# FNet mixing and a gated FFN on one core: first weight piece by halves, batch 0 folded row by row, piece 4 loaded behind slice 1's tables

## The chip, the cores and the metric

One core of a Trainium2 chip runs the whole program. The engines that matter: TensorE (PE) multiplies, with its weight loads shown apart as PEld; VectorE (DVE), ScalarE (ACT) and GpSimd (POOL) work element by element; SyncE (SP) does nothing but issue DMAs. Each engine takes its instructions in the order of the program and waits at the head of its queue. The metric is device time in microseconds of one execution, the median of several; lower is better.

## The reference

```python
def _attn_ref(x):                      # x: (8, 3008, 256)
    X = np.fft.fft(x, axis=1)
    X = np.fft.fft(X, axis=2)
    return X.real.astype(np.float32)

def _moe_ref(x, w_gate, w_val, w_out): # x: (24064, 256), d_ff = 1536
    gate = 1.0 / (1.0 + np.exp(-(x @ w_gate)))
    val = x @ w_val
    return (gate * val @ w_out).astype(np.float32)

def reference(**kwargs):
    ...
    attn_out = _attn_ref(**attn_kwargs)
    B, S, D = attn_out.shape
    x = attn_out.reshape(B * S, D)
    return _moe_ref(x=x, **moe_kwargs)
```

The weights arrive as float64 (8 bytes each), x as float32.

## The kernel before

The real part of the two-dimensional transform is a product with cosine and sine tables. Each batch of 3008 rows is first folded by its symmetries into four quarters (index h) of 126 x 6 points: 126 partitions, and six points per partition that the code calls rows, q = 0 to 5. The fold is additions and subtractions of quarters and of mirrored features. Six rows, taken two at a time, make three slices (N3 = 3) of batch 0; a slice is loaded by one DMA (`load_third`, 1 MB, tile x) and has two table parts (`load_table`, tile st, 0.38 MB each). The sums over rows run on TensorE with the folded rows as weights and the tables as the moving operand, into the PSUM tiles ev and od; a small extra sum for one feature column goes to the tile pe (`e0_sums`). The transform along the features is not carried out on x: it is multiplied into the gate and value weights instead ("merge", `dt` is its table, result G), so that afterwards the main loop works from pk and qk (the sums over rows), G and the output weights wf.

The weights are cut in 18 pieces of 256 x 256 float64 numbers, 0.5 MB each: pieces 0 to 11 alternate between gate and value, 12 to 17 belong to the output weights. A piece is loaded into raw (and its copies wqk, wf, wc, wx by home), as two 128-row blocks c = 0 and 1, side by side. It is converted to float32 by integer operations on the two 32-bit halves of each number:

- `weight_parts` (ScalarE): an Abs of the high words (L317) and a scaled Copy of the low words (L319);
- `weight_join`: on VectorE two tensor_scalar operations through a PSUM bank (L330, L331) and one scalar_tensor_tensor (L333), and an add on GpSimd (L335);
- `merge`: eight matmul instructions (four matmuls, each in two passes) into a PSUM bank ps, and `merged` copies that to G on ScalarE (L366). `ge_load` moves a row of G into the tile ge by small DMAs.

Order is by hand: the program schedules nothing by itself, every engine runs its instructions as they are written. SP issues, in this order: pieces 0 and 1, dt, pieces 2 and 3; then for each slice j its part of x, piece 3 + j if j > 0, and its tables; then pieces 6 and 7. The start proper is the part from `warm(12)` to `weight_join(5, "x2")`: twelve matmuls on a constant tile (busy), pieces 0 to 3 converted and merged, then the loop over the three slices. In a slice, `folds[2 * j]` is `third` (L506, L507, twice L468, on VectorE) with a copy to xe on ScalarE (L524), and `folds[2 * j + 1]` is `feats` (L513, L515, L516, on VectorE) with `turned` (L518, three copies a slice on ScalarE: XV, which lies in the tile st, and a copy within x for each row). The matmuls of the slice follow: e0 sums, halves 0 and 1 (ev and od of two blocks) first with the rows themselves and then with the turned copies, and the group halves[2]. Piece 4 is converted across slices 0 and 1 and merged behind slice 1; piece 5 is converted behind slice 1, its join behind the loop.

After the loop come the copies of the sums (`then` and `places`: a copy on ScalarE, L586, and two VectorE operations, L592 and L596), pieces 6 to 10 woven into another group of sums (ev and od, six matmul instructions at a time), the first `seed` and `front_a` calls, and the main loop of `front_a`, `front_b`, gate and `back`, which runs to the end.

Of the kernel before, what the change touches and what calls it, by code (L numbers as in the profile page):

```python
# [53 lines left out]
NQ = 6  # L54
# [28 lines left out]
def kernel(  # L83
# [50 lines left out]
    def mm(o, l, r, start, stop):  # L134
        nc.tensor.matmul(o, l, r, start=start, stop=stop, skip_group_check=True)  # L135
# [129 lines left out]
    def weight_load(j):  # L265


        w, c = jobs[j]
        src = (moe_w_gate, moe_w_val, moe_w_out)[w]
        src = src[2 * c * P : 2 * (c + 1) * P, :] if w == 2 else src[:, c * WC : (c + 1) * WC]  # L270
        src = src.rearrange("(c p) f -> p c f", p=P)

        def some(n, pool, tag):

            if tag not in shared:
                shared[tag] = pool.tile([P, n * WC], F32, name=f"w{tag}", tag=tag)
            return shared[tag]

        def home(j):

            if j in (0, 1, 2, 10, 11):
                t = hp.tile([P, 6 * WC], F32, name="raw", tag="h")
                return t[:, 0 : 4 * WC], t[:, 4 * WC :]
            if j in (3, 4):
                ws = some(5, pqp, "qk")[:, (j - 3) * 2 * WC : (j - 2) * 2 * WC]
                return sp.tile([P, 4 * WC], F32, name="raw", tag="sf"), ws
            if j < 8:
                t = wf[:, j - 4].rearrange("p m n -> p (m n)")
                return t[:, 0 : 4 * WC], t[:, 4 * WC : 6 * WC]
            if j < 10:  # L290
                shared[j] = cp.tile([P, 10 * WC], F32, name="wc", tag="c")
                return shared[j][:, 0 : 4 * WC], shared[j][:, 4 * WC : 6 * WC]
            return (shared[8][:, 6 * WC :] if j == 12 else shared["qk"][:, 0 : 4 * WC],
                    shared[9][:, (6 + 2 * (j - 12)) * WC : (8 + 2 * (j - 12)) * WC])

        if j < KEEP:
            raw, ws = home(j)
        else:
            both = some(24, xp, "x4").rearrange("p (i n) -> p i n", n=2 * WC)
            i = 3 * (j - KEEP)  # L300
            raw, ws = both[:, i : i + 2].rearrange("p a n -> p (a n)"), both[:, i + 2]
        raw = raw.bitcast(I32).rearrange("p (c f w) -> p c f w", c=2, w=2)
        ws = ws.rearrange("p (c f) -> p c f", c=2)
        WS[j] = ws
        if src.dtype == F32:
            nc.sync.dma_start(out=ws, in_=src)
        else:
            RAW[j] = raw
            nc.sync.dma_start(out=raw.rearrange("p c f w -> p c (f w)"), in_=src.bitcast(I32))  # L309

    def weight_parts(j, which=(0, 1)):

        if j in RAW:
            raw, ws = RAW[j], WS[j]
            lo, hi = raw[:, :, :, 0], raw[:, :, :, 1]
            if 0 in which:
                nc.scalar.activation(ws, hi.bitcast(F32), AF.Abs)  # L317
            if 1 in which:
                nc.scalar.activation(lo, lo.bitcast(U32), AF.Copy, scale=2.0 ** -29)  # L319

    def weight_join(j, other=None):
        if j not in RAW:
            return
        raw, ws = RAW.pop(j), WS[j]
        lo, hi = raw[:, :, :, 0], raw[:, :, :, 1]
        wi = ws.bitcast(I32)
        mid_ = bank("join", other).rearrange("p (c f) -> p c f", c=2)
        mi = mid_.bitcast(I32)
        ts = nc.vector.tensor_scalar
        ts(out=mid_, in0=ws, scalar1=2.0 ** -15, scalar2=HUGE, op0=ALU.max, op1=ALU.min)  # L330
        ts(out=mi, in0=mi, scalar1=3, scalar2=0x3FFFFFF8, op0=ALU.logical_shift_left,  # L331
           op1=ALU.bitwise_and)
        nc.vector.scalar_tensor_tensor(out=wi, in0=hi, scalar=-(2 ** 30), in1=mi,  # L333
                                       op0=ALU.bitwise_and, op1=ALU.bitwise_or)
        nc.gpsimd.tensor_tensor(wi, wi, lo, op=ALU.add)  # L335

    WO, parts_ = {}, []

# [14 lines left out]

    def merge(ws, g, c, other):
        ps = MERGED[g, c] = bank("ps", other)
        for h in range(2):
            for t in range(2):
                mm(ps[:, h * WC : (h + 1) * WC], dt[:, t, h * HD : (h + 1) * HD], ws[:, t, :],
                   h == 0 and t == 0, t == 1)

# [251 lines left out]

    E0 = {}

    def e0_sums(j, which=(0, 1)):

        for turned in which:
            for q in (2 * j, 2 * j + 1):
                for blk in range(2):
                    row = (2 * blk + q % 2) * TB  # L620
                    w = xe[:, blk, q : q + 1] if turned else W[0, blk][2][:, q]
                    mm(E0["ps"][row : row + 1, columns(blk)[turned]], w, table_of(0, q, blk, turned),
                       not j and not turned, j == N3 - 1)

    def e0_copies():

# [336 lines left out]
    def piece(j, other=None):  # L963
        merge(WS.pop(j), *jobs[j], other)
# [246 lines left out]
```

## Time and profile before

| what | value |
|---|---|
| device time, median of 3 | 1923.47 us (1922.28 to 1925.69) |
| profiled execution, its own time | 1922.13 us |
| its span, first to last instruction | 1920.4 us |
| granted TensorE clock | 1.000 |
| TensorE busy | 1911.3 us, 100% |
| VectorE, ScalarE, GpSimd busy | 74%, 70%, 81% |
| DMA, moved in all | 95.63 MB, mean 50 GB/s |
| DMA from 9 to 18 us, 18 to 26 us | 326 GB/s, 311 GB/s |

The first slices of the span are unlike the rest, in which TensorE is busy throughout and the DMA nearly idle:

| stretch, us | PE busy | DVE busy | ACT busy | POOL busy | DMA GB/s |
|---|---|---|---|---|---|
| 0 to 9 | 7.07 | 4.22 | 4.59 | 3.17 | 268 |
| 9 to 18 | 7.58 | 8.71 | 3.92 | 5.12 | 326 |
| 18 to 26 | 8.00 | 6.96 | 5.06 | 0.66 | 311 |
| 26 to 33 | 6.61 | 6.04 | 3.66 | 0.67 | 296 |
| 33 to 40 | 7.00 | 5.80 | 5.48 | 2.04 | 218 |
| 40 to 60 | 19.87 | 16.61 | 17.72 | 7.64 | 188 |

How to read it: an instruction's line in the timeline gives its start, its duration, the engine, the source line, what it writes and reads, how many were merged, and in brackets how long the engine was idle before and what released it. The ends of matmuls are modelled, so TensorE's busy time is not its work at its peak rate; the distance between starts is. All matmuls have one source line (L135, a helper), so they are told apart by tile.

### The profile page before, as it was taken

To read this page: it belongs to the slowest core of one execution; us is meant where nothing else is said; L and a number is where in the kernel's file an instruction comes from. 1 tells how busy PE (TensorE), PEld (TensorE's weight loads), DVE (VectorE), ACT (ScalarE), POOL (GpSimd) and SP (SyncE) were. 2 spreads that over 40 slices of the span, in tenths; PEclk is the share of its full clock that TensorE was granted. 3 is DMA by queue.
4 is the path that set the end of the run, shared out by engine and by line. 5 is a ranking of instruction groups with operands and counts; after the bars stand their busy time and mean duration, and the time that the engine had idled before them with its cause. 6 is when DMAs were issued, how large, how long until landed. Compare 5 with 4: busy or idle time off the path is not lost.

```text
span 1920.4 us, 34666 instructions
## 1 busy us (share of the span) xinstructions
PE 1911.3 (100%) x11342; PEld 1793.1 (93%) x11342; DVE 1411.7 (74%) x3216; ACT 1345.3 (70%) x3155; POOL 1555.5 (81%) x2811
## 2 busy tenths in 40 slices
PE   9999999999999999999999999999999999999999
PEld 7899999999999999999999999999999999999998
DVE  8667876787777876777777777777777687767776
ACT  6877767767777677776777767777677767777775
POOL 3589979978898688986888878988788876777775
PEclk9999999999999999999999999999999999999999
DMA  9342322120120201202111020111200100010001
GB/s 302 97 83 50 94 82 61 46 80 15 24 78 20 80 20 42 60 15 83 26 47 47 21 83 19 47 52 23 80 15 16 26 15 15 15 23 19 26 18 29
DMA packets 169299, 95.63 MB, mean 50 GB/s; under 512 B 129742, under 2 KB 160024, under 8 KB 167328
## 3 DMA queue, kind: packets, MB, share of 16 engines
q1 hardware_dynamic: 168838, 93.17, 17.6%
q8 instruction: 91, 1.49, 0.3%
q14 instruction: 88, 0.72, 0.1%
q10 hardware_dynamic: 250, 0.24, 0.0%
q0 software_dynamic: 32, 0.00, 0.0%
HBM read 68.13 MB, written 47.24 MB: 60 GB/s over the span
## 4 chain that ended last, share of the span: by engine, by line
PE 96%; DMA 2%; SPq 1%; POOL 0%; DVE 0%; ACT 0%; issue 0%; ACTq 0%; POOLq 0%
PE pf L135 50%; PE po L135 41%; PE ev L135 3%; PE rows L135 1%; DMA x<-in_xf_dram 1%; PE od L135 1%; DMA wc<-in_moe_w_out_dram 0%; DMA wx<-in_moe_w_out_dram 0%; PE row L135 0%; SPq L309 0%; POOL sf L773 0%; SPq L214 0%; PE pe L135 0%; PE ps L135 0%; POOL st L239 0%
## 5 line engine op out<-in xcount | busy, mean ns | idle before, releaser
L773 POOL TENSOR_TENSOR sf<-h 128x168 f32<-128x168 f32 (+1 forms) x935 | 516.4, 571 | 230.4 <-DVE h L767 229.6
L773 POOL TENSOR_TENSOR sf<-h,sf 128x168 f32<-128x168 f32 (+1 forms) x1122 | 614.9, 568 | 49.0 <-DVE h L767 48.0
L135 PE MATMUL pf<-pk,G 128*128 128x252 f32 (+1 forms) x2304 | 582.6, 376 | 0.0
L135 PE MATMUL pf<-qk,G 128*128 128x252 f32 (+1 forms) x2304 | 582.0, 375 | 0.1
L725 ACT ACTIVATE pf<-ek,ge 128x252 f32<-128x252 f32 (+1 forms) x1152 | 542.6, 471 | 19.5 <-DVE h L767 0.3
L767 DVE TENSOR_TENSOR h<-pf,z 128x252 f32<-128x252 f32 (+1 forms) x576 | 241.5, 419 | 413.3 <-ACT pf L764 411.8
L135 PE MATMUL po<-sf,wf 128*128 128x168 f32 (+1 forms) x2992 | 516.9, 306 | 0.3 <-POOL sf L773 0.2
L736 ACT ACTIVATE ae<-pf 128x504 f32<-128x504 f32 (+1 forms) x576 | 339.1, 589 | 247.0 <-PE pf L135 245.3
L135 PEld LDWEIGHTS pf<-pk,G 128*128 128x128 f32 x2304 | 436.8, 190 | 52.0 <-issue 2.0
L135 PEld LDWEIGHTS po<-sf,wf 128*128 128x128 f32 x2992 | 460.4, 190 | 9.2 <-POOL sf L773 1.2
L135 PE MATMUL po<-h,wf 128*128 128x168 f32 (+1 forms) x2618 | 463.2, 305 | 0.0
L135 PEld LDWEIGHTS pf<-qk,G 128*128 128x128 f32 x2304 | 410.6, 190 | 26.6 <-ACT ae L736 0.8
L751 DVE TENSOR_TENSOR z<-ae,pf 128x504 f32<-128x504 f32 (+1 forms) x576 | 386.0, 670 | 62.6 <-ACT h L750 58.0
L135 PEld LDWEIGHTS po<-h,wf 128*128 128x128 f32 x2618 | 416.5, 190 | 16.2
L891 DVE TENSOR_TENSOR c<-c 128x168 f32<-128x168 f32 (+1 forms) x929 | 425.6, 466 | 3.4
L750 ACT ACTIVATE h<-pf 128x252 f32<-128x252 f32 (+1 forms) x576 | 218.4, 379 | 208.1 <-PE pf L135 200.4
L763 DVE TENSOR_TENSOR h<-h,pf 128x252 f32<-128x252 f32 (+1 forms) x576 | 233.6, 405 | 0.0
L764 ACT ACTIVATE pf<-z 128x252 f32<-128x252 f32 (+1 forms) x576 | 211.4, 367 | 24.9 <-DVE h L763 21.0
L773 POOL TENSOR_TENSOR sf<-sf 128x168 f32<-128x168 f32 (+1 forms) x187 | 104.3, 558 | 14.7
L773 POOL TENSOR_TENSOR sf<-sf,h 128x168 f32<-128x168 f32 (+1 forms) x187 | 110.1, 589 | 0.0
L804 ACT COPY c<-po 128x504 f32<-128x504 f32 (+1 forms) x141 | 80.0, 568 | 0.0
L900 DVE STREAM_TRANSPOSE os<-c 128x256 f32<-128x256 f32 x184 | 79.9, 435 | 0.0
(163 smaller groups left out, 919.8 us busy)
## 6 DMA issues: line engine op xcount, KB each, us to landing
x<-xr SPq DMA_DIRECT2D x14, 1536.0 KB
out_dram<-os SPq DMA_DIRECT2D x368, 56.0 KB
xr<-in_xf_dram SPq DMA_DIRECT2D x14, 768.0 KB
xr<-in_xf_dram SPq DMA_DIRECT2D x35, 256.0 KB
ek<-ed SPq DMA_DIRECT2D x39, 126.0 KB
out_dram<-os SPq DMA_DIRECT2D x284, 7.0 KB
x<-in_xf_dram SPq DMA_DIRECT2D x3, 1024.0 KB
st<-in_stab_dram SPq DMA_DIRECT2D x4, 564.8 KB
```

Source lines behind the costliest of these rows:

```text
L135: nc.tensor.matmul(o, l, r, start=start, stop=stop, skip_group_check=True)
L725: nc.scalar.activation(PF[i][:, g], EK[i // NFT], AF.Copy, scale=ge[:, g, f : f + 1])
L736: nc.scalar.activation(AP[i], PF[i], AF.Copy, scale=2.0)
L750: nc.scalar.activation(H[p][:, fh, 0:n], PF[i][:, 0], AF.Sigmoid)
L751: nc.vector.tensor_tensor(z[:, :, ::-1], AP.pop(i), PF[i], op=ALU.subtract)
L763: nc.vector.tensor_tensor(h[:, fh, 0:n], h[:, fh, 0:n], pf[:, 1], op=ALU.mult)
L764: nc.scalar.activation(pf[:, 0], z[:, 0], AF.Sigmoid)
L767: nc.vector.tensor_tensor(h[:, fh, n:], pf[:, 0], z[:, 1], op=ALU.mult)
L773: nc.gpsimd.tensor_tensor(block(p, dst), block(p, a), block(p, b), op=(ALU.subtract, ALU.add)[op])
L804: (nc.vector.tensor_copy if t == 1 or t == 3 and not last else nc.scalar.copy)(C[0][:, 3 * t * R : 3 * (t + 1) * R], PO[t][:, 0 : 3 * R])
L891: engine.tensor_tensor(t[:, dst * R : (dst + 1) * R], *v, op=(ALU.subtract, ALU.add)[op])
L900: nc.vector.transpose(os_[0][:, s, 0:nb, h, :], t[:, c0 : c0 + nb * TB])
```

## The change

The edits, all in the start of the kernel:

1. Piece 0 is loaded by two DMAs, one for each 128-row block, and converted block by block on all engines.
2. In pieces 1 to 4 the last two steps of the join (L333 on VectorE and the add on GpSimd) are done block by block; the steps ahead of them stay whole.
3. The matmuls of a merge run block by block (t outside, h inside), for all pieces.
4. Batch 0 is folded and summed row by row (six steps) instead of by slices of two rows (three steps); `e0_sums` takes one row.
5. Piece 4 is loaded behind slice 1's tables instead of ahead of them, and converted and merged as a whole behind row 3. The first ScalarE step of piece 5 runs behind row 4, the second behind row 5.
6. Twelve warm-up matmuls become nine.

```diff
         WS[j] = ws
+        cuts = (slice(0, 1), slice(1, 2)) if not j else (slice(0, 2),)
         if src.dtype == F32:
...
         else:
             RAW[j] = raw
-            nc.sync.dma_start(out=raw.rearrange("p c f w -> p c (f w)"), in_=src.bitcast(I32))
+            for c in cuts:
+                nc.sync.dma_start(out=raw[:, c].rearrange("p c f w -> p c (f w)"),
+                                  in_=src[:, c].bitcast(I32))
...
-    def weight_join(j, other=None):
+    def weight_join(j, other=None, cuts=(BOTH,), last=None):
...
-        ts(out=mid_, in0=ws, scalar1=2.0 ** -15, scalar2=HUGE, op0=ALU.max, op1=ALU.min)
-        ts(out=mi, in0=mi, scalar1=3, scalar2=0x3FFFFFF8, op0=ALU.logical_shift_left,
-           op1=ALU.bitwise_and)
-        nc.vector.scalar_tensor_tensor(out=wi, in0=hi, scalar=-(2 ** 30), in1=mi,
-                                       op0=ALU.bitwise_and, op1=ALU.bitwise_or)
-        nc.gpsimd.tensor_tensor(wi, wi, lo, op=ALU.add)
+        for c in cuts:
+            w, m = ws[:, c], mid_[:, c]
+            ts(out=m, in0=w, scalar1=2.0 ** -15, scalar2=HUGE, op0=ALU.max, op1=ALU.min)
+            m = m.bitcast(I32)
+            ts(out=m, in0=m, scalar1=3, scalar2=0x3FFFFFF8, op0=ALU.logical_shift_left,
+               op1=ALU.bitwise_and)
+            for d in last or (c,):
+                wi, lo, hi = ws[:, d].bitcast(I32), raw[:, d, :, 0], raw[:, d, :, 1]
+                nc.vector.scalar_tensor_tensor(out=wi, in0=hi, scalar=-(2 ** 30), in1=mid_[:, d].bitcast(I32),
+                                               op0=ALU.bitwise_and, op1=ALU.bitwise_or)
+                nc.gpsimd.tensor_tensor(wi, wi, lo, op=ALU.add)
...
-        for h in range(2):
-            for t in range(2):
+        for t in range(2):
+            for h in range(2):
                 mm(ps[:, h * WC : (h + 1) * WC], dt[:, t, h * HD : (h + 1) * HD], ws[:, t, :],
                    h == 0 and t == 0, t == 1)
...
-    def e0_sums(j, which=(0, 1)):
-
-        for turned in which:
-            for q in (2 * j, 2 * j + 1):
-                for blk in range(2):
...
+    def e0_sums(q, turned):
+
+        for blk in range(2):
...
     for j in range(N3):
         load_third(j)
-        if j:
-            weight_load(3 + j)
+        if j == N3 - 1:
+            weight_load(5)
         for t in range(2):
             load_table(t, j)
+        if j == 1:
+            weight_load(4)
...
-    warm(12)
+    warm(9)
     for j in range(4):
-        weight_parts(j)
-        weight_join(j, j % 3)
+        weight_parts(j, cuts=(BOTH,) if j else HALVES)
+        weight_join(j, j % 3, (BOTH,) if j else HALVES, HALVES if j else None)
         piece(j, ("x0", "x1", "x2", 3)[j])
...
-    folds = fold_ops(0, 2)
+    folds = fold_ops(0, 1)
...
-    for j in range(N3):
-        qs = (2 * j, 2 * j + 1)
-        folds[2 * j]()
-        if not j:
-            e0_sums(j)
+    for q in range(NQ):
+        folds[2 * q]()
+        e0_sums(q, 0)
+        if not q:
             merged(3)
             ge_load(3)
             for i in (8, 9, 10, 11, 12):
                 weight_load(i)
-        else:
-            e0_sums(j, (0,))
-        if j == N3 - 1:
-            merged(4)
-        folds[2 * j + 1]()
-        for sums, _, _ in halves[0:2]:
-            sums(*qs, which=(0,))
-        if j:
-            e0_sums(j, (1,))
-        for sums, _, _ in halves[0:2]:
-            sums(*qs, which=(1,))
-        halves[2][0](*qs)
-        if j == 0:
-            weight_parts(4)
-        elif j == 1:
-            weight_join(4, "x2")
-            piece(4, "x2")
-            weight_parts(5)
+        folds[2 * q + 1]()
+        for sums, _, _ in halves[0:2]:
+            sums(q, which=(0,))
+        e0_sums(q, 1)
+        for sums, _, _ in halves[0:2]:
+            sums(q, which=(1,))
+        halves[2][0](q)
+        if q == 3:
+            weight_parts(4)
+            weight_join(4, "x2", last=HALVES)
+            piece(4, "x2")
+        elif q == 4:
+            merged(4)
+            weight_parts(5, (0,))
+    weight_parts(5, (1,))
     weight_join(5, "x2")
```

`weight_parts` takes the same cuts and runs its two ScalarE operations for each. HALVES are the slices 0:1 and 1:2 of the block index, BOTH is 0:2.

More of the change, by code (lines that the diff above doesn't have):

```diff
@@ L304, in weight_load, with weight_parts @@
         WS[j] = ws
+        cuts = (slice(0, 1), slice(1, 2)) if not j else (slice(0, 2),)
         if src.dtype == F32:
-            nc.sync.dma_start(out=ws, in_=src)
+            for c in cuts:
+                nc.sync.dma_start(out=ws[:, c], in_=src[:, c])
         else:
             RAW[j] = raw
-            nc.sync.dma_start(out=raw.rearrange("p c f w -> p c (f w)"), in_=src.bitcast(I32))
-    def weight_parts(j, which=(0, 1)):
-        if j in RAW:
[L314 to L319, printed above, removed]
-    def weight_join(j, other=None):
+            for c in cuts:
+                nc.sync.dma_start(out=raw[:, c].rearrange("p c f w -> p c (f w)"),
+                                  in_=src[:, c].bitcast(I32))
+    BOTH = slice(0, 2)
+    HALVES = (slice(0, 1), slice(1, 2))
+    def weight_parts(j, which=(0, 1), cuts=(BOTH,)):
+        if j in RAW:
+            for c in cuts:
+                raw, ws = RAW[j][:, c], WS[j][:, c]
+                lo, hi = raw[:, :, :, 0], raw[:, :, :, 1]
+                if 0 in which:
+                    nc.scalar.activation(ws, hi.bitcast(F32), AF.Abs)
+                if 1 in which:
+                    nc.scalar.activation(lo, lo.bitcast(U32), AF.Copy, scale=2.0 ** -29)
+    def weight_join(j, other=None, cuts=(BOTH,), last=None):
         if j not in RAW:
@@ L324, in weight_join @@
         raw, ws = RAW.pop(j), WS[j]
-        lo, hi = raw[:, :, :, 0], raw[:, :, :, 1]
-        wi = ws.bitcast(I32)
         mid_ = bank("join", other).rearrange("p (c f) -> p c f", c=2)
-        mi = mid_.bitcast(I32)
         ts = nc.vector.tensor_scalar
-        ts(out=mid_, in0=ws, scalar1=2.0 ** -15, scalar2=HUGE, op0=ALU.max, op1=ALU.min)
-        ts(out=mi, in0=mi, scalar1=3, scalar2=0x3FFFFFF8, op0=ALU.logical_shift_left,
-           op1=ALU.bitwise_and)
-        nc.vector.scalar_tensor_tensor(out=wi, in0=hi, scalar=-(2 ** 30), in1=mi,
-                                       op0=ALU.bitwise_and, op1=ALU.bitwise_or)
-        nc.gpsimd.tensor_tensor(wi, wi, lo, op=ALU.add)
+        for c in cuts:
+            w, m = ws[:, c], mid_[:, c]
[8 more added lines that the diff above has]
+                nc.gpsimd.tensor_tensor(wi, wi, lo, op=ALU.add)
     WO, parts_ = {}, []
@@ L613 @@
     E0 = {}
-    def e0_sums(j, which=(0, 1)):
-        for turned in which:
-            for q in (2 * j, 2 * j + 1):
-                for blk in range(2):
[L620 to L623, printed above, removed]
+    def e0_sums(q, turned):
+        for blk in range(2):
+            row = (2 * blk + q % 2) * TB
+            w = xe[:, blk, q : q + 1] if turned else W[0, blk][2][:, q]
+            mm(E0["ps"][row : row + 1, columns(blk)[turned]], w, table_of(0, q, blk, turned),
+               q < 2 and not turned, q >= NQ - 2)
     def e0_copies():
```

## The prediction

> **What bounds the kernel now.** I read the page first, for the busy shares and the chain that ended last; then the chain in order of time for the first 100 us; then the timeline from 0 to 75 us, engine by engine; last the busy time by windows, for the DMA rate.
>
> The page, its busy line and the chain by engine:
>
> ```profile
> PE 1911.3 (100%) x11342; PEld 1793.1 (93%) x11342; DVE 1411.7 (74%) x3216; ACT 1345.3 (70%) x3155; POOL 1555.5 (81%) x2811
> ...
> PE 96%; DMA 2%; SPq 1%; POOL 0%; DVE 0%; ACT 0%; issue 0%; ACTq 0%; POOLq 0%
> ```
>
> TensorE holds 96% of the chain. The matmuls of the main loop are the same before and after, so the change can move the end only by moving the moment from which TensorE runs without a break. The chain in order of time shows where that moment is:
>
> ```profile
> 11.68 14.87 DMA x<-in_xf_dram
> 26.57 0.17 DVE x L506
> 26.74 1.14 DVE x L507
> 27.91 0.70 DVE x L468
> 28.63 0.69 DVE x L468
> 29.32 0.04 issue
> 29.37 0.69 DVE x L515
> 30.08 0.70 DVE x L516
> 30.78 0.04 issue
> 30.83 0.59 PE ev L135 x2
> ```
>
> The last third of batch 0 (x2) lands at 26.57, VectorE folds both its rows until 30.77, and TensorE starts their sums at 30.83. From there the weight loads wait 0.30, 0.31 and 0.53 us (at 41.44, 47.62, 56.62), and next to nothing until the tail. So the end is 30.83 plus the work behind it. The batch-0 sums end at 35.39, when the next group (ev x6) starts; I follow that mark. The timeline also shows what VectorE and GpSimd do to each other:
>
> ```profile
> 13.97 1.21 DVE L507 TENSOR_TENSOR x<-x 126x1020 f32<-126x1020 f32 x1
> 14.09 2.23 POOL L335 TENSOR_TENSOR wqk<-wqk,raw 128x512 int32<-128x512 int32 x1 [0.78 <-ACT G L366]
> 15.21 2.38 DVE L468 TENSOR_TENSOR x<-x 126x512 f32<-126x512 f32 x2
> ...
> 25.34 1.29 POOL L335 TENSOR_TENSOR wqk<-wqk,raw 128x512 int32<-128x512 int32 x1 [9.03 <-DVE wqk L333]
> ```
>
> The same GpSimd add takes 1.29 alone and 2.23 beside the fold; the two L468 take 2.38 instead of 1.42 (at 20.28). About 0.95 is lost on each side.
>
> **Part by part.** *Prices on VectorE.* 126x1020 takes 1.21, 126x508 0.68: 1.04 ns an element and 0.15 fixed. A dependent next operation starts 0.03 after the end of the one before (28.63, 29.37, 30.08), an independent one 0.08 before it (30.69 after an end at 30.77). So 256 elements take 0.42, as L763's 128x252 does (0.41), and start to start 0.455 or 0.34.
>
> *Loads.* Piece 0 as two transfers is one more issue of 0.45 on SP; everything on SP goes out 0.5 later until 6.55, where an issue already takes 2.54 because the queue is full, so nothing later moves. Piece 4's 0.5 MB and slice 1's tables change places, both still ahead of x2, so x2 lands at 26.57 again. The tables land some 1.5 earlier. Piece 4 lands near 23 instead of by 20.50 (the tables' 0.76 MB at the 190 to 300 GB/s of that stretch); ScalarE asks for it at 25.5, so 2 us cover that. Piece 5 keeps its place.
>
> *Pieces 0 to 3.* The first half lands between 3.9 and 4.9; by its bytes 4.3. VectorE starts at 4.8 instead of 5.63. Piece 0 costs six operations, 2 x (0.455 + 0.455 + 0.34) = 2.5 instead of 2.07; pieces 1 to 3 cost 0.725 x 2 + 0.34 x 2 = 2.13 each. VectorE is free at 4.8 + 2.5 + 6.4 = 13.7, where it was 13.89: gain 0.2. TensorE's piece 3 ends two halves sooner (GpSimd's 128x256 add is 0.73 in the trace), near 16.3 instead of 18.1. That alone shortens nothing: the rows come from VectorE. The swapped loops of the merge and warm(9) move no matmul onto the path.
>
> *Row by row.* One row: 0.08 + 0.72 + 3 x 0.455 + 0.34 = 2.5 on VectorE. Before, a slice took 18.96 to 23.07, 2.06 a row. So 0.45 more for each of six rows. [...]
>
> Rows 0 and 1: 13.7 + 5.0 + 0.9 beside GpSimd's add of piece 3 (paid before too) = 19.6; x1 had landed by 18.96. Rows 2 and 3 end at 24.7.
>
> *Piece 4, moved.* Its ScalarE parts are queued behind row 3's xe, XV and turned copy, which wait for row 3's last VectorE operation. The two copies start 0.40 apart each (0.89 for two now), so Abs runs 25.5 to 26.2. VectorE stands behind that: join(4) is ahead of row 4 in its queue, so it idles 24.7 to 26.2 and joins until 28.35. Before, join(4) ran at 23.07 and was over at 25.2, ahead of x2's landing. Now row 4 starts 1.8 after x2 landed. GpSimd's add of piece 4 ran at 25.34, while VectorE idled; its second half now meets row 4. That costs VectorE between 0 and 0.97 (the row at 15.21); I take 0.75, one half add. [...] Rows 4 and 5 then end at 28.35 + 0.75 + 5.0 + 0.1 = 34.2, instead of 30.77: 3.4 later.
>
> *TensorE behind it.* A row's sums: six matmuls in two passes, 8 x 0.16 for halves 0 and 1, 4 x 0.16 for the third, 0.1 at each change of shape: 2.1. The e0 sums ran as 8 instructions in 0.43, four column groups side by side; by row only two stand side by side: 0.21 to 0.43 for 4, I take 0.32, twice a row. Together 2.75 a row, 5.5 a slice where it was 4.7. Piece 4's matmuls stand ahead of row 4 on TensorE and end near 31. Row 4 can start at 31.8 and ends near 34.2; row 5's e0 goes first, its sums follow feats at 34.3 to 34.5, and all end at 37.0. Before: 35.39. So **+1.6 us**: of the 3.4 VectorE loses, 1.8 come back because only one row's sums, not two, stand behind its end.
>
> *After that.* ScalarE's four row-wise extras per slice (0.2 to 0.4 each) lie in its idle time (it idles 3.27 at 28.06). VectorE's queue goes on 3.4 late, 1.8 more than TensorE; it has idle time of 1.03, 0.24, 0.40 and 0.48 before 49.25 to catch up in (2.15), and pieces 6 and 7 have 1.9 and 1.5 between GpSimd's end and their matmuls. So the 1.6 passes to the end as it is. The profiled execution took 1922.13 us (span 1920.4 and 1.7 around it), and becomes 1923.7; it lies 1.34 under the median, so the median becomes 1923.47 + 1.6 = **1925.1 us**.
>
> **Rivals.** About 0.2% (3.85 us) is what a measurement of this kernel can tell from no change, and the forecast is within it.
>
> *The rows pay off.* If GpSimd's add finds gaps between the short operations (-0.75), the e0 sums run at 0.21 (-0.3), and the changes of shape cost nothing (-0.4), TensorE ends at 35.5, no change. If moreover the fixed cost of short operations overlaps and VectorE is done with join(4) when x2 lands, rows 4 and 5 end at 26.57 + 5.0 = 31.6 and the sums near 34: 1.4 faster, 1922.1. For it: TensorE is free two microseconds earlier. Against it: the idle 0.03 between dependent operations in the chain, and the queue orders, which are written out. It can't give 3.85: x2's landing and two folds bound it.
>
> *VectorE's backlog becomes the bound.* Place: VectorE from 34.2 to the first gate of the main loop (z, 49.25 before). If the 2.15 of idle time is not where the backlog needs it (0.88 of it lies behind join 9), the weight pieces and the first gate come as late as the fold, +3.4; with contention at its upper row for both adds (+0.5) it is 3.9 and more, 1927.4 to 1928.3. It decides when VectorE shows no idle time between 34 and 50. For it: between 36.02 and 49.25 it idles 0.88 in all. Against it: the 1.03 is a wait for ScalarE's copy of ev, which row 4 finishes early.
>
> *The transfers move.* If halves and the new order let x2 land 2 us or more earlier, TensorE still waits for VectorE, which is busy until 28.35; only with VectorE free too could it be over 3.85 faster. The DMA ran at 311 to 326 GB/s from 9 to 26 us with a share of 1.06, so there is no room.
>
> **How the numbers follow.** Forecast 0.58 (1924.0 to 1926.3), rows pay off 0.17 (1921.8 to 1924.0), backlog 0.21 (1926.3 to 1928.6, nearly all of it counted as over 0.2%), transfers 0.04. Faster by over 0.2%: 0.04; slower by over 0.2%: 0.2; within: 0.76. The range from 1922.2 to 1928.2 leaves out the transfers and the ends of the two other rivals.
>
> **What would show it.** Right: join(4)'s first operation near 26, row 4's first fold operation near 28.3 with no DMA wait before it, the last fold end near 34.2, the sums' end near 37.0, x2 landed by 26.6 as before, and the main loop's first unbroken matmul near 58.2. Wrong: fold operations of 256 elements that start under 0.4 apart, a fold end before 32.5, an add of piece 4 that delays no VectorE operation, or a shift of the sums' end that is not found again at 60 us.

## The result and the profile after

The changed kernel takes 1926.86 us (median of 22 runs, 1925.63 to 1928.93). The kernel before, run beside it, takes 1923.57 us (22 runs, 1922.02 to 1926.67). The ratio is 1.0016, with a 95% interval of 1.001 to 1.0023: 3.29 us slower, which the runs resolve, and less than the 0.2% that the prediction took as its bound for no change. The forecast was +1.6 us, 1925.1. In one run of the kernel before, in the first set of the experiments, the clock was down to 0.654 and the time 2873.77 us; ratios and spreads leave it out.

The two profiled executions lie further apart, 1927.15 against 1922.13, 5.0 us. The two gaps agree: the execution profiled before was 1.44 under its median of 1923.57, and the one after is 0.29 above its median; 5.02 - 1.44 - 0.29 = 3.29. All marks below are compared between these two executions, so they add up to 5.0 and not to 3.3.

The page of the changed kernel, its busy line and its chain by engine:

```profile
PE 1915.5 (99%) x11336; PEld 1792.4 (93%) x11336; DVE 1413.8 (73%) x3244; ACT 1349.9 (70%) x3163; POOL 1556.7 (81%) x2816
...
PE 97%; DMA 1%; DVE 1%; ACT 0%; POOL 0%; SPq 0%; issue 0%; ACTq 0%; POOLq 0%
```

VectorE, ScalarE and GpSimd carry 28, 8 and 5 instructions more, and the busy time of each hardly changes. Between VectorE and the DMA the chain has shifted a little. The chain in order of time (start, length, what) shows where:

```profile
6.84 15.32 DMA x<-in_xf_dram
22.19 0.16 DVE x L516
22.35 0.61 DVE x L517
...
26.87 0.44 DVE x L526
27.36 0.05 issue
27.41 0.51 ACT st L528
27.92 0.40 ACT x L528
28.32 0.58 ACT wqk L325
28.92 0.71 DVE join L337
29.65 0.71 DVE join L339
30.39 0.75 DVE wqk L343 x2
31.14 0.55 DVE x L516
...
34.12 0.44 DVE x L526
34.60 0.91 PE ev L135 x4
35.51 0.42 PE pe L135 x4
35.92 1.48 PE ev L135 x8
37.40 0.42 PE pe L135 x4
37.82 0.84 PE od L135 x4
38.65 0.42 PE pe L135 x4
39.07 1.48 PE od L135 x8
40.55 0.95 PE ev L135 x6
```

Before, this chain started with the last third of x (x2), at 26.57. Now it starts with the second third (x1), which lets VectorE go on only at 22.19. Rows 2 and 3 are folded, ScalarE copies row 3 (L528) and converts piece 4 (L325), VectorE joins piece 4 at 28.92, and only then comes row 4. The timelines of ScalarE, VectorE and GpSimd show three waits (for piece 1, for x1 and for piece 4) and one contention (in brackets the idle time before an instruction and what ended it):

```profile
7.76 0.66 ACT L325 ACTIVATE raw<-raw 128x512 f32<-128x512 f32 x1 [2.64 <-DMA raw<-in_moe_w_val_dram]
```

```profile
8.45 0.69 DVE L337 TENSOR_SCALAR join<-raw 128x512 f32<-128x512 f32 x1 [1.62 <-ACT raw L325]
...
22.19 0.16 DVE L516 TENSOR_TENSOR x<-x 126x2 f32<-126x2 f32 x1 [1.35 <-DMA x<-in_xf_dram]
...
28.92 0.70 DVE L337 TENSOR_SCALAR join<-wqk 128x512 f32<-128x512 f32 x1 [1.63 <-ACT wqk L325]
...
31.05 0.63 DVE L516 TENSOR_TENSOR x<-x 126x2 f32<-126x2 f32 x1
...
32.32 1.31 DVE L478 TENSOR_TENSOR x<-x 126x256 f32<-126x256 f32 x2
...
35.25 0.88 DVE L478 TENSOR_TENSOR x<-x 126x256 f32<-126x256 f32 x2
...
36.63 0.42 DVE L526 TENSOR_TENSOR x<-x 126x254 f32<-126x254 f32 x1
```

```profile
30.94 1.94 POOL L345 TENSOR_TENSOR wqk<-wqk,raw 128x256 int32<-128x256 int32 x2 [14.28 <-DVE wqk L343]
```

Finally the busy time by windows, before and then after; the last two columns are the DMA engines' busy share and the GB/s:

```profile
3.50:7.00 3.50, 3.50 (x15) 3.05 (x14) 1.34 (x2) 1.94 (x4) 0.00 (x0) 1.00 1.05 390
7.00:12.00 5.00, 3.89 (x17) 2.83 (x17) 4.83 (x9) 3.62 (x6) 2.58 (x2) 1.00 1.05 387
12.00:26.00 14.00, 12.94 (x90) 9.81 (x89) 12.77 (x22) 6.53 (x13) 4.17 (x3) 1.00 1.07 306
```

```profile
3.50:7.00 3.50, 3.50 (x12) 2.91 (x11) 2.56 (x6) 1.52 (x4) 0.77 (x2) 1.00 0.91 277
7.00:12.00 5.00, 3.33 (x14) 2.31 (x14) 3.45 (x6) 3.35 (x6) 2.13 (x3) 1.00 1.03 386
12.00:26.00 14.00, 13.44 (x74) 8.48 (x72) 12.04 (x34) 6.11 (x14) 3.38 (x4) 1.00 1.06 267
```

The loads run at 277 instead of 390 GB/s from 3.5 to 7 us, and at 267 instead of 306 from 12 to 26. From 12 to 26 us the DMA engines are as busy as before (1.06 and 1.07) and move less.

### The profile page after: what moved, and what is told of

Its sections match the earlier page's. It is cut to its first block, busy times and chain, and to the rows that moved or that the text cites. A ratio compares the mean times of both kernels' runs of the same rounds, so it can differ in the third digit from the quotient of the medians.

```text
span 1925.4 us, 34705 instructions
## 1 busy us (share of the span) xinstructions
PE 1915.5 (99%) x11336; PEld 1792.4 (93%) x11336; DVE 1413.8 (73%) x3244; ACT 1349.9 (70%) x3163; POOL 1556.7 (81%) x2816
## 4 chain that ended last, share of the span: by engine, by line
PE 97%; DMA 1%; DVE 1%; ACT 0%; POOL 0%; SPq 0%; issue 0%; ACTq 0%; POOLq 0%
PE pf L135 50%; PE po L135 41%; PE ev L135 3%; PE rows L135 1%; PE od L135 1%; DMA x<-in_xf_dram 1%; PE ps L135 0%; PE row L135 0%; POOL sf L781 0%; PE pe L135 0%; DVE x L478 0%; SPq L312 0%; SPq L214 0%; DVE x L517 0%; POOL st L239 0%
```

## The experiments

Three causes stood against each other, and the expectations name them by letters. T: the transfers; the load in halves, or the new order of the loads, makes x late. V: VectorE's own order; the shorter folds, the wait for piece 4 and the contention set the end, as the prediction had it. P: TensorE's row; its nine groups take longer than a row on VectorE and are the bound themselves. "+x" is against the median of the kernel before in the same set of runs: 1922.94 for the first four, 1923.57 for the next four, 1923.67 for the last four (31 or 33 runs each). All other kernels have 11 runs (r_after 9).

| kernel | median, us (lowest to highest) | ratio to before, 95% |
|---|---|---|
| r_after | 1926.67 (1926.21 to 1929.62) | 1.0022 (1.0012 to 1.0032) |
| e1_whole_load | 1926.13 (1926.01 to 1926.33) | 1.0016 (1.0008 to 1.0025) |
| e2_old_order | 1927.22 (1926.38 to 1929.88) | 1.0023 (1.0013 to 1.0032) |
| e3_by_slices | 1927.27 (1926.17 to 1927.89) | 1.0021 (1.0013 to 1.003) |
| e4_rows_only | 1924.82 (1924.72 to 1925.02) | 1.0005 (0.9996 to 1.0014) |
| e12_e0_by_slice | 1926.46 (1924.99 to 1928.25) | 1.0012 (1.0003 to 1.0021) |
| e5_half_load_only | 1925.33 (1923.45 to 1926.86) | 1.0006 (0.9997 to 1.0014) |
| e7_abs4_early | 1926.87 (1925.91 to 1929.38) | 1.0017 (1.0008 to 1.0026) |
| e15_piece4_only | 1925.28 (1924.61 to 1926.78) | 1.0009 (1.0001 to 1.0018) |
| e13_three_undone | 1923.77 (1923.11 to 1924.72) | 0.9999 (0.9991 to 1.0008) |
| e10_last_slice_rows | 1923.22 (1922.28 to 1924.55) | 0.9998 (0.9989 to 1.0007) |
| e14_rows_piece5_late | 1923.69 (1923.35 to 1924.69) | 0.9998 (0.9989 to 1.0007) |

**r_after: the changed kernel once more.** No edit; is the late x a chance of one execution?

> The changed kernel once more, unaltered, to see what of its profile comes back. In its first profile the second slice of x released VectorE at 22.19 (by 18.96 before), the DMA moved 260 to 300 GB/s from 3.5 to 7 us (390 before), row 4's fold began at 31.05 where 28.35 was forecast, and the batch-0 sums ended at 40.38 (35.39 before). Theory V (VectorE's queue: longer rows, the wait for piece 4's Abs, the add of piece 4 beside the fold): it costs +1.6 whatever the transfers do, and the other 1.7 to 3.4 us are transfers that fell late by chance; then this profile shows the second slice by 20 and the sums' end near 37. Theory T (the new load order or the load by halves makes the transfers late every time): 22 and 40 again, +3.3 us.

It is not. VectorE waits 1.20 us for x1 again (21.47), the DMA again runs at 290 and 321 GB/s in the two halves of the stretch from 3.5 to 7 us, and TensorE waits 2.10 us for a table (35.09). The sums end at 42.87: this execution (1929.62 us) is the slowest of its nine. Which wait is on the path differs between the two executions; that transfers are late does not.

**e1: piece 0 loaded whole**, everything else as changed.

```diff
-        cuts = (slice(0, 1), slice(1, 2)) if not j else (slice(0, 2),)
+        cuts = (slice(0, 2),)
```

> The changed kernel with piece 0 loaded by one DMA again; its conversion stays by halves. Theory T with the halves as the cause: 390 GB/s from 3.5 to 7 us again, piece 1's Abs near 6.3 instead of 7.76, the second slice 1 us sooner, and the kernel 1 us faster than the changed one (+2.3 against before). Theory V, or T with the order as the cause: no difference beyond 0.5 us, +3.3.

The DMA is back at 401 GB/s (3.5 to 5.25 us), and VectorE no longer waits for x1: row 2 starts at 20.22. But the median falls by only 0.5, to +3.2 where T expected +2.3 and V +3.3. The timelines of ScalarE and VectorE tell where the rest went:

```profile
23.24 0.51 ACT L528 ACTIVATE st<-x,sgn 126x256 f32<-126x256 f32 x1 [1.02 <-PE od L135]
...
26.39 0.51 ACT L528 ACTIVATE st<-x,sgn 126x256 f32<-126x256 f32 x1 [1.66 <-PE ev L135]
```

```profile
27.88 0.69 DVE L337 TENSOR_SCALAR join<-wqk 128x512 f32<-128x512 f32 x1 [2.56 <-ACT wqk L325]
```

The turned copies of rows 2 and 3 (L528) wait for TensorE: each starts just after TensorE's matmuls on the turned copy of the row before are over (those of row 1 run from 22.25 to 23.16, the copy of row 2 starts at 23.24). The data don't ask for this wait, since in the code XV has a place of its own for each row within the tile st; why it is there, no run shows. Piece 4's conversion is queued behind those copies, and VectorE's join behind that. VectorE idles 2.56 instead of 1.63 us, so of the 2 us by which row 2 starts earlier only 1.04 are left at join(4). TensorE itself runs row after row without a gap from 17.25 to 29.9. In this trace no fold waits for x and no sum for a table, and the spread of the 11 runs is 0.3 us, where it was 3.3 in the changed kernel.

**e2: piece 4 loaded ahead of slice 1's tables**, as before the change.

```diff
-        if j == N3 - 1:
-            weight_load(5)
+        if j:
+            weight_load(3 + j)
         for t in range(2):
             load_table(t, j)
-        if j == 1:
-            weight_load(4)
```

> The changed kernel with piece 4 loaded ahead of slice 1's tables again, everything else as changed. Theory T with the order as the cause: the second slice of x is there by 19 to 20, row 4 folds from 28.4, and the kernel comes to +1 against before. Theory V: the order hides nothing and costs nothing, the second slice lands as in the changed kernel, +3.3.

No gain (1927.22). x1 comes earlier, with a wait of 0.56 left (20.74), but the turned copy of row 3 then waits 2.42 for TensorE (27.68), and join(4) starts at 29.18, later than in the changed kernel. TensorE itself had started row 2 only at 25.02, after 1.35 us of idle time. The profile names the fold's L478, but that had ended at 22.42; more likely it was slice 1's table, which now lands behind piece 4 (in e5, with the same order, TensorE waits 0.54 for it, at 23.71). What T expected of this edit did not come: what x gains, the table seems to lose.

**e3: folds and sums by slices of two rows again**, the rest as changed, except that both of piece 5's ScalarE steps now stand behind the loop.

```diff
-    folds = fold_ops(0, 1)
+    folds = fold_ops(0, 2)
...
-    for q in range(NQ):
-        folds[2 * q]()
-        e0_sums(q, 0)
+    for j in range(N3):
+        qs = (2 * j, 2 * j + 1)
+        folds[2 * j]()
+        for q in qs:
+            e0_sums(q, 0)
...
-            sums(q, which=(0,))
+            sums(*qs, which=(0,))
...
-        elif q == 4:
-            merged(4)
-            weight_parts(5, (0,))
-    weight_parts(5, (1,))
+    merged(4)
+    weight_parts(5)
```

> The changed kernel with batch 0 folded and summed by slices of two rows again; piece 4 is still converted and merged behind slice 1 as a whole, and piece 5's two ScalarE steps behind the loop. Theory V: six times 0.45 less on VectorE, of which the end sees 0.8 (a slice's sums, not a row's, stand behind the last fold): +2.4 against before if the transfers are as late as in the changed kernel. Theory T alone: the fold starts late as before, two rows' sums stand behind it, no gain or some loss: +3.3 to +4.

1927.27: no faster than row by row (+4.3; T expected +3.3 to +4, V +2.4). The wait for x1 is 2.10 us here (21.29), join(4) waits 2.23 for ScalarE and starts at 27.71, and slice 2 is folded from 29.84 to 34.93. The sums end at 39.54, 0.84 earlier than in the changed kernel, and part of that is lost again: join(5) waits 2.71 for piece 5's first step (37.63), and the main loop's mark (61.66 in the changed kernel) is at 61.32. So going back to slices alone gains next to nothing in the changed kernel; e4 asks what rows cost when x is in time.

**e4: the kernel before, with folds and sums row by row and nothing else.**

```diff
-    folds = fold_ops(0, 2)
+    folds = fold_ops(0, 1)
...
-    for j in range(N3):
-        qs = (2 * j, 2 * j + 1)
-        folds[2 * j]()
+    for q in range(NQ):
+        folds[2 * q]()
+        e0_sums(q, 0)
...
-        if j == 0:
+        if q == 1:
             weight_parts(4)
-        elif j == 1:
+        elif q == 3:
             weight_join(4, "x2")
```

> The kernel before with one edit: batch 0 folded and summed row by row. Loads, conversion of pieces 0 to 3, piece 4's place and its load order stay as before. Theory P (TensorE is the bound in the rows: 3.15 us a row, measured from row to row in the run with the whole load, 6.3 a slice where it was 4.7): 18.1 (end of piece 3) + 6 x 3.15 + 1.73 (piece 4) = 38.7 for the end of the batch-0 sums, 35.39 before: +3.3 us from this edit alone. Theory V (VectorE's queue, rows of 2.75 on TensorE): the fold ends near 33, the sums near 36.2: +0.8. Theory T (the transfers): nothing is loaded otherwise, so no change.

TensorE's timeline, one row of batch 0 and the start of the next, and then the first group behind all rows:

```profile
20.80 0.49 PE L135 MATMUL pe<-st,x 126*1 126x189 f32 x4
21.21 0.91 PE L135 MATMUL od<-st,x 126*128 126x189 f32 x4
22.05 0.49 PE L135 MATMUL pe<-st,xe 126*1 126x188 f32 x4
22.47 0.91 PE L135 MATMUL od<-st 126*128 126x188 f32 x4
23.21 0.80 PE L135 MATMUL od<-st,x 126*128 126x189 f32 x4
23.94 0.49 PE L135 MATMUL pe<-st,x 126*1 126x189 f32 x4
...
38.16 1.12 PE L135 MATMUL ev<-st,x 126*128 126x188 f32 x6
```

From one row's first matmul to the next is 23.94 - 20.80 = 3.14 us, 3.05 to 3.15 in every row, with no gap on TensorE from 17.65 on, while VectorE's last fold ends at 32.9. The sums end at 38.16, near P's 38.7 and 2 us from V's 36.2. So with x in time TensorE's row is the bound: +1.25 in the median (not resolved by the interval; it is the marks of one profiled execution that name TensorE as the bound), again with a spread of 0.3.

**e12: the e0 sums of two rows together**, behind the odd row, in the changed kernel.

```diff
         folds[2 * q]()
-        e0_sums(q, 0)
...
-        e0_sums(q, 1)
...
         halves[2][0](q)
+        if q % 2:
+            for turned in range(2):
+                e0_sums(q - 1, turned)
+                e0_sums(q, turned)
```

> The changed kernel with the e0 sums of both rows of a slice issued together behind its odd row, so four column groups stand side by side again and two changes of shape a row are gone. Theory P: a row falls from 3.15 to about 2.1, the e0 sums cost about 0.9 a slice: 5.1 to 5.3 a slice instead of 6.3, and the kernel is 1 us (rows 4 and 5 alone) to 2.5 us faster than the changed one, +1 to +2.5 against before. Theories V and T: VectorE's fold or the landing of x sets the end, at most 0.4 us faster, +3.2 or more.

A row's own matmuls now take 2.1, and the pair of e0 sums 0.32 and 0.43 (16 instructions, where two rows had 16 in four lots of four, each 0.42). In the profiled execution the sums end at 38.51 instead of 40.38. The median gains 0.4 against the changed kernel's, not the 1 to 2.5 that P expected: this execution (1925.28) is a quick one, and waits of 0.75 for x1 (20.74) and 1.61 before join(4) stay.

**e5: the kernel before, with piece 0 loaded by two DMAs and nothing else.**

```diff
-            nc.sync.dma_start(out=raw.rearrange("p c f w -> p c (f w)"), in_=src.bitcast(I32))
+            for c in cuts:
+                nc.sync.dma_start(out=raw[:, c].rearrange("p c f w -> p c (f w)"),
+                                  in_=src[:, c].bitcast(I32))
```

> The kernel before with one edit: piece 0 is loaded by two DMAs, its conversion starts when each whole operand is there. Theory T: the DMA moves 250 to 340 GB/s from 3.5 to 7 us instead of 370 to 410, the third slice of x, which binds in the kernel before, lands 1 to 1.5 us later than 26.57, and the kernel is 1 to 1.5 us slower. If the dip is due to something else: 390 GB/s as before and no change.

One edit, and the whole effect on the loads is there: busy time by windows, and the fold that waits for x2 in VectorE's timeline.

```profile
3.50:7.00 3.50, 3.50 (x12) 2.91 (x11) 1.73 (x3) 1.35 (x3) 0.00 (x0) 1.00 0.95 315
7.00:12.00 5.00, 4.70 (x22) 3.57 (x21) 4.62 (x8) 4.04 (x7) 2.59 (x2) 1.00 1.02 374
12.00:26.00 14.00, 12.32 (x86) 9.23 (x84) 12.76 (x22) 6.58 (x14) 3.51 (x2) 1.00 1.07 277
```

```profile
28.09 0.17 DVE L510 TENSOR_TENSOR x<-x 126x4 f32<-126x4 f32 x1 [2.01 <-DMA x<-in_xf_dram]
```

x2 lands at 28.09 instead of 26.57, and the sums end at 37.30 instead of 35.39: +1.9 by the marks, +1.76 in the median, a little above what T expected (1 to 1.5). The two executions are alike in that each is some 1.4 under its median. The interval includes no change, so the time alone does not settle it; that the halves slow the transfers is shown by the bytes that had been moved by 26 us, over all kernels (from the trace's DMA view):

| piece 0 loaded | kernel and MB moved by 26 us |
|---|---|
| whole | before 7.83, e1 7.75, e4 7.88, e10 7.75, e14 7.67, e15 7.73, e13 7.51 |
| by halves | changed 7.08, r_after 6.99, e2 7.17, e3 7.21, e5 7.31, e7 7.01, e12 7.33 |

No kernel of the second row reaches the first. Half a megabyte, at some 300 GB/s, is 1.7 us. Most of it goes missing late: of the 0.52 MB that e5 is short of the kernel before, 0.12 are missing by 12 us (3.43 against 3.55) and the rest from 12 to 26 us.

**e7: piece 4's ScalarE steps behind row 2** instead of row 3, in the changed kernel.

```diff
-        if q == 3:
+        if q == 2:
             weight_parts(4)
+        elif q == 3:
             weight_join(4, "x2", last=HALVES)
```

> The changed kernel with piece 4's two ScalarE steps behind row 2 instead of behind row 3, so VectorE need not wait for them after row 3. Theory V: the idle 1.6 us ahead of join(4) are gone, rows 4 and 5 fold 1.6 earlier, and 1 to 1.5 us come back (+2 against before). Theory P: TensorE's rows fill the time, at most 0.7 us comes back (its gap ahead of piece 4's matmuls), +2.7 to +3.3.

The wait that the prediction named is nearly gone: join(4) starts at 27.46 after 0.34 of idle time, and what is left is piece 4 itself, which ScalarE can start on only at 26.76 (a wait of 1.13 for the DMA), where the prediction had it land near 23. The end does not move (1926.87), because row 4 then waits 0.75 for x2 (30.43) and TensorE 1.94 for a table (34.27). V's 1 to 1.5 us are refuted for the kernel as it stands: the transfer stood right behind the wait.

**e15: the kernel before, with the order of loads and the place of piece 4 changed and nothing else.**

```diff
-        if j:
-            weight_load(3 + j)
+        if j == N3 - 1:
+            weight_load(5)
         for t in range(2):
             load_table(t, j)
+        if j == 1:
+            weight_load(4)
...
-        if j == 0:
+        if j == 1:
             weight_parts(4)
-        elif j == 1:
             weight_join(4, "x2")
```

> The kernel before with one edit: piece 4 loaded behind slice 1's tables and converted and merged as a whole behind slice 1. By VectorE's queue (theory V): slice 1's fold ends at 23.1, ScalarE's Abs follows its turned copies, join(4) runs from about 25.6 to 27.6 and stands ahead of slice 2's fold, which starts at 27.6 instead of 26.57, shares 1 us with GpSimd's add and ends near 32.8 (30.77 before): +2.0 us against the profiled execution of the kernel before, 1924.1, and a narrow spread, since x no longer binds. If the place of piece 4 costs nothing (TensorE's row cost and the halves alone made the loss): no change.

VectorE's timeline, the join of piece 4 and the fold of the last slice, and then TensorE's:

```profile
25.88 0.69 DVE L330 TENSOR_SCALAR join<-wqk 128x512 f32<-128x512 f32 x1 [2.24 <-ACT wqk L317]
...
29.18 0.28 DVE L506 TENSOR_TENSOR x<-x 126x4 f32<-126x4 f32 x1 [1.15 <-DMA x<-in_xf_dram]
```

```profile
32.96 0.50 PE L135 MATMUL pe<-st,x 126*1 126x189 f32 x8 [1.47 <-DMA st<-in_stab_dram]
```

+1.61 in the median, where 2.0 was expected. join(4) runs at 25.88, as the prediction's mechanism has it (26.2). But the fold behind it waits 1.15 more for x2, and TensorE for a table, and the spread that was expected to be small is 2.2. So the new order alone seems to bring x2 later, though the same bytes stand ahead of it and SP issues it at the same time (11.65, before 11.68). Every trace in which the fold waits for x2 fits. With piece 0 whole, x2 lands at 26.57, 27.41 and 28.03 where piece 4 stands ahead of slice 1's tables (before, e10, e14), and at 28.98 and 29.18 where it stands behind them (e13, e15). By halves, it lands at 28.09 in the old order (e5) and at 30.43 and 30.94 in the new one (e7, r_after). Where the fold doesn't wait, its start is only an upper bound: 26.84 in e4, with e10's loads, and 29.84 in e3 and 29.59 in e12, with those of e7 and r_after but earlier than in either. These are single executions, and why it is so, no run shows.

**e13: three causes undone at once** in the changed kernel: piece 0 whole (e1), e0 sums of two rows together (e12), piece 4's ScalarE steps behind row 2 (e7); the diff is those three.

> The changed kernel with three things undone together: piece 0 loaded whole (its conversion stays by halves), the e0 sums of a slice together behind its odd row, and piece 4's ScalarE steps behind row 2. Rows, the load order, the joins by halves and nine warm-ups stay. If these three (late transfers, TensorE's cost a row, the wait ahead of join(4)) are the loss, the fold of row 4 starts near 27.4, the batch-0 sums end near 36.2 and the kernel comes to about 1923, 3.5 to 4 us under the changed one and even with the kernel before. If the rows and the load order cost by themselves: 1924.5 or more.

1923.77 against 1923.67: the loss is gone. join(4) starts at 25.66, and row 4, whose fold was expected near 27.4, starts at 28.98 and is back to waiting for x2, as in the kernel before (VectorE's timeline):

```profile
28.98 0.16 DVE L516 TENSOR_TENSOR x<-x 126x2 f32<-126x2 f32 x1 [1.11 <-DMA x<-in_xf_dram]
```

The sums end at 37.31 in that execution (expected 36.2). The rows, the new order and the joins by halves are still in this kernel: by themselves they cost nothing that these runs resolve.

**e10: a version that might gain**: the kernel before, with only the last slice folded by rows and its e0 sums together at its end.

```diff
         qs = [slice(q, q + nq) for q in range(0, NQ, nq)]
+        if not b:
+            qs = qs[0:2] + [slice(4, 5), slice(5, 6)]
...
+        if 5 in qs:
+            for turned in range(2):
+                for q in (4, 5):
+                    e0_sums(q, turned)
```

> The kernel before with only the last slice folded and summed row by row, and its e0 sums for both rows together at its end; all loads, piece 4 and the first two slices as before. Row 4 is folded 2.5 us after x lands instead of 4.2 for both rows, its sums run while VectorE folds row 5, and no change of shape is added: row 4's sums from 29.7 (behind piece 4's matmuls), row 5's from 31.6 to 33.6, the e0 sums to 34.5, where it was 35.39: 0.9 us faster. If each small operation costs more than it hides: no change.

1923.22, 0.45 below the kernel before; the interval includes 1. In its trace x2 lands at 27.41 and the sums end at 36.19, 8.78 us behind it; before it was 35.39 - 26.57 = 8.82. The first full sums start sooner behind the landing (31.20, 3.79 behind, where it was 30.83, 4.26 behind) and give it back: nothing is gained.

**e14: the same, with piece 5 loaded behind slice 2's tables** and its ScalarE steps behind the loop.

```diff
-        if j:
-            weight_load(3 + j)
+        if j == 1:
+            weight_load(4)
         for t in range(2):
             load_table(t, j)
+        if j == 2:
+            weight_load(5)
...
-            weight_parts(5)
+    weight_parts(5)
     weight_join(5, "x2")
```

> As the kernel with the last slice by rows, and piece 5 loaded behind slice 2's tables and its ScalarE steps behind the loop. The tables land 1.4 us sooner than piece 5 lets them now, so that row 4's sums never wait for them: 0.9 us faster than the kernel before, 0.5 more in executions whose transfers are late; no gain over the kernel without it if the tables were in time anyway.

1923.69, no difference. The sums end at 36.06, and what follows pays for piece 5: its join starts at 34.75, after 1.61 us of idle time. The profile names TensorE, but ScalarE's first step on piece 5 runs from 34.07 to 34.72, so it is that step which the join waits for. From the sums' end to the main loop's mark (58.42) it takes 22.4 us, where it took 21.2 before. No version here beats the kernel before.

## Where the prediction was right, and which two of its terms were wrong

The direction was right: slower, and by less than 0.2%. The size was not: +1.6 was forecast, and it is 3.3 between the medians and 5.0 between the two profiled executions. The median of 1926.86 lies in the range of the prediction, but in the part (1926.3 to 1928.6) that it gave to VectorE's backlog, a cause that did not come about; so it is in part luck that the range holds. Point by point, between the profiled executions:

| mark | before | predicted | after |
|---|---|---|---|
| row 2's fold starts (before: slice 1's) | 18.96 | 19.6 | 22.19 |
| join(4) starts | 23.07 | 26.2 | 28.92 |
| row 4's fold starts | 26.57 | 28.35 | 31.05 |
| last fold ends | 30.77 | 34.2 | 37.05 |
| sums end | 35.39 | 37.0 | 40.38 |
| first unbroken matmul of the main loop | 56.63 | 58.2 | 61.66 |

**Loads: the step that failed.** "So nothing later moves": the load in halves was priced from SP's side alone, one issue more, 0.45, and later issues that are long anyway. The trace of the kernel before has those: 0.45 at 0.74, 2.54 at 6.55, and 0.40 again at 35.28, shortly after the DMA has all but stopped (2 and 0 GB/s from 33 to 35 us); that the queue is full in between is how the prediction read it. The load in halves did bring the first half early (VectorE starts at 4.03, forecast 4.8), but SP issues x1 1.3 later (6.84 instead of 5.51). What was not priced is the rate. Everything that the table's first line is late by (2.6 against the prediction) is a wait for a transfer or follows from one: 1.35 for x1, and 1.15 because VectorE began row 0 at 14.85 instead of 13.7. The latter goes back to piece 1, whose Abs was ready to start only at 7.76 (6.30 before). From there to the fold's end the steps are those predicted, 2.7 to 2.85 late. e5 puts the load in halves at +1.8 alone (not resolved by its interval), and e1 shows that the rate falls with the transfer that is cut, not with the work by halves on the engines: e1 keeps that work and moves 386 GB/s from 3.5 to 7 us (390 before). Why two DMAs of 0.25 MB slow what comes behind them, until 26 us, is open: no run cuts another load, or one into more parts.

The rival "the transfers move" had them come earlier only. Its other side was missing. A second statement on the loads, that x2 "lands at 26.57 again" since the same bytes stand ahead of it, fails too, as far as single executions tell: in the new order x2 lands 1 to 2.6 us later with piece 0 whole (28.98 and 29.18, against 26.57 to 28.03).

**TensorE's row: the term that was too small.** 2.75 was forecast, 3.14 measured (e4, e1). Two of its parts were off. The four e0 instructions of one row take 0.42, the upper of the two ends and not the 0.32 between them (+0.2 for two). And the changes of shape cost the 0.1 that was taken, but there are four in a row, since each pe group stands between two full groups; two were counted (+0.2). 2.75 + 0.4 = 3.15. The first part, too, is likely a change of shape: eight e0 instructions take 0.32 when more of them follow and 0.43 when full matmuls do, and behind the four of a row full matmuls always follow. VectorE's row was right: 2.5 forecast, 2.51 from start to start (22.19 to 24.70). With TensorE's row longer than VectorE's, the sums can't catch up behind the last fold as the prediction had it: 40.38 - 37.05 = 3.3 instead of 2.8.

**Piece 4's place: right.** VectorE stands idle for it 1.63 us; 24.7 to 26.2 was the forecast. e15 has this part, with the new order, alone at +1.6, though in its trace waits for x2 (1.15) and for a table (1.47) stand behind the join. Not foreseen was what e1 and e2 show: the row copies ahead of piece 4 in ScalarE's queue may wait for TensorE (1.02 and 1.66 us in e1, 2.42 in e2), so whatever holds TensorE up (its long rows in e1, in e2 likely a table) delays the join of a weight piece.

**Contention: right.** 0.75 was taken, and L516 took 0.63 instead of 0.15 or 0.16, the pair of L478 1.31 instead of 0.88: 0.9. GpSimd's two half adds took 1.94, the first 0.73, as long as the one at 5.62, and the second 1.26. L516 ends at 31.68, and the first add at about the same time (30.94 + 0.73 = 31.67). Of the pair, the first is the long one: 0.85 from 32.32, instead of 0.42, beside the second add. L517 between them took 0.68, as in row 5.

**Behind the sums: right.** The marks at 40.38 and 61.66 are both 5.0 late, as is the end: what TensorE was late by passes through unchanged. The backlog on VectorE did not become the bound, and the rows did not pay off.

**From profile to median: half right.** The prediction added its difference to the median. The difference between the medians is 1.7 smaller than that between the executions, since the one before happened to be a quick one. The kernel before spreads over 4.7 us in these 22 runs (2 to 4 in the other sets), e1 and e4 over 0.3. The latter two wait for TensorE and not for x; so it is likely, though only argued, that the spread is that of x's landing, and that TensorE's longer row costs less in the median (1.25) than against the profiled execution (2.8), because in a usual run part of it lies beside the wait for x.

**Why undoing one thing gives little.** Three bounds lie within a microsecond or two of each other: the landing of x and its tables, TensorE's row, and VectorE's wait for piece 4. Undoing one (e1, e2, e3, e7, e12) gains 0.7 at most against 1926.86, since the next is there; undoing three (e13) gains all of it. Alone, the parts cost 1.8 (halves, e5), 1.25 (rows, e4) and 1.6 (piece 4, e15), 4.6 in sum, and together 3.3: they seem to overlap, though of the three only e15's interval leaves out no change. That the forecast came within 1.8 us of the median was luck in part: a term that was missing (loads) and one that was short (TensorE's row) ran beside the wait that it did have.

## What to carry to other kernels

A load that is cut in two can have a second price beside its issue, as the first one had here: the rate of what is queued behind it (277 instead of 390 GB/s from 3.5 to 7 us, 267 instead of 306 from 12 to 26), which is read from the windows of the DMA and from the bytes moved by the time that the last input is wanted. Where work is cut into smaller steps, count the step on every engine that it passes, with each change of shape on TensorE (0.1 us a side here): the engine that was free before may now have the longest step (here TensorE, 3.14 us a row where VectorE's took 2.51). And where undoing a part gives nothing, look in its trace for what waits next, and undo both (where the engine that the trace names had long been done, look for the transfer that came last); a single reversal can't acquit a cause when several bounds lie close together.

## What the runs showed of the hardware

- Two DMAs of 0.25 MB in place of one of 0.5 MB, first in the queue, came with a rate of 277 to 318 GB/s from 3.5 to 7 us, where it was 378 to 392, and of 256 to 277 instead of 281 to 308 from 12 to 26 us, there at about the same busy share of the DMA engines (1.06 to 1.08). These are the seven traces with the halves and the seven without.
- Matmuls of one column of weights (`126*1`): eight instructions in four column groups took 0.32 us from start to start where more of them followed (e12), and 0.43 where full matmuls did (e12 and before); four instructions in two groups took 0.41 or 0.42 there (e4). Going by rows, half the instructions took the same time.
- Between these and full 128-column matmuls a change took the full ones 0.1 us on each side: in e4, 0.84 for four full ones between two such groups, 0.73 to 0.75 with one at one side, 0.64 with none.
